# A cached attention layer beside a squared-ReLU layer: two heads a load in 64 KB rows, three places in place of ten

## The chip, the core and the metric

The kernel runs on one of the eight cores of a Trainium2 chip, as one program. The metric is device time in microseconds (us) from launch to end; lower is better. A core has five engines that run side by side, each through its own list of instructions in order: TensorE (PE, matrix products, with its loads of weights as PEld), VectorE (DVE), ScalarE (ACT), GpSimd (POOL) and SyncE (SP, which here only issues transfers). Engines wait for each other by semaphores. Transfers between HBM and the on-chip memory SBUF run on 16 DMA engines. SBUF has 128 partitions; a tile is an array of 128 rows, one in each. Matrix products end up in PSUM.

## The reference

Two tokens (B = 2, one position each) of D = 448 pass through two branches that a gate mixes. Branch A is attention of 16 heads with 256 elements over a cache of 4096 keys and values; branch B is a dense layer with a squared ReLU, 448 to 1792 to 448. All is float32.

```python
g = sigmoid((x * gate_w).sum(-1, keepdims=True))
q = (x @ wq).reshape(B, Sq, H, Dh).transpose(0, 2, 1, 3)
scores = einsum("bhqd,bhkd->bhqk", q, k_cache) * (Dh ** -0.5)
p = softmax(scores, axis=-1)
a = einsum("bhqk,bhkd->bhqd", p, v_cache).transpose(...).reshape(B, Sq, H * Dh) @ wo
h = einsum("bsd,df->bsf", x, w1) + b1
r = where(h > 0, h, 0)
b = einsum("bsf,fd->bsd", r * r, w2) + b2
out = g * a + (1 - g) * b
```

The caches are the bulk of the data: 2 x 16 x 4096 x 256 numbers of 4 bytes, twice, are 268.4 MB. wq and wo are 7.34 MB each, w1 and w2 3.21 MB each.

## The kernel before

**Places.** One pool named `ring` has 10 places of 16 KB a partition (`RING = 10`, `slot`, L54 and L67). Every large load goes to the next place in turn, so it waits until the tile that stood there ten loads earlier has been used up. Almost all loads are 2 MB: 128 rows of 16 KB.

**Order of the loads.** SP issues all large loads, in the order of the program: wq in four pieces (L73), then, pair by pair, keys and values. A pair is one token and one head; there are 32 of them, the two tokens of a head behind each other (`pairs`, L133). The keys of a pair are two loads, its values two more (`load_kv`, L121). In a round i the kernel loads the keys of pair i + 1, then the values of pair i. The weights are strewn in between: w1 at i = 2, half of w2 at i = 4, a quarter of wo at every fourth head, the rest of w2 at the very end. SP also waits at each load for the load eight before it.

**Scores** run on DVE: `times_q` (L268) multiplies 16 keys a partition with the query in place, `row_sums` (L275) sums each key's 256 products. The query lies in all partitions: `make_q` (L218) spreads a row with a matrix product and ACT copies it.

**Softmax** of a pair: DVE takes the maximum m of each partition (L283), PE spreads the 128 maxima to all partitions (mt, L285), DVE takes the maximum of those (nb, L291), ACT computes the exponentials with their sums (L294). While PE makes mt, DVE already multiplies the first four keys of the next pair (`LEAD = 4`). After the second token of a head, PE adds the sums over the partitions and DVE turns them into factors rl (`norm`, L302).

**Values**: `values` (L311) is 16 matrix products of 4 x 512 for a pair, in four column groups of PE, that add up in `po_buf`. [...] `turn` (L320) brings the result of a head into columns, `project` (L333) multiplies it with wo into `acc`.

**Second branch**: `ffn_hidden` (PE and ACT) runs in round 3 behind the values, `ffn_square` (DVE) in round 3 behind the scores of the next pair; the first half of w2 is added to `acc` in round 5, the second half at the end of the program. The end (L406 to L416) adds, behind the last head, five pieces of w2 and the last two blocks of wo to `fin` with narrow products (`late`, L338), copies and writes.

Of the kernel before, what the change touches and what calls it, by code (L numbers as in the profile page):

```python
# [13 lines left out]


@with_exitstack
def kernel(
    ctx: ExitStack,
    tc: tile.TileContext,
    x: bass.AP,  # L20
    k_cache: bass.AP,
    v_cache: bass.AP,
    wq: bass.AP,
    wo: bass.AP,
    w1: bass.AP,
    b1: bass.AP,
    w2: bass.AP,
    b2: bass.AP,
    gate_w: bass.AP,
    out: bass.AP,  # L30
):
    nc = tc.nc
    P = 128
    B, H, S, DH = k_cache.shape
    D = x.shape[-1]
    F = w1.shape[1]
    N = H * DH
    CF = D // P
    R0 = CF * P
    RR = D - R0  # L40
    assert 2 * RR == P and B == 2
    NK = S // P
    J = 16
    NCH = NK // J
    HG = 4
    NG = H // HG
    FC = F // P
    FB = F // D
    NJ = DH // P
    QB = 512  # L50
    NQ = N // QB
    QH = QB // DH
    DQ = D // 4
    RING = 10  # L54
    WH = FC // 2
    LEAD = 4
# [3 lines left out]
    ring = ctx.enter_context(tc.tile_pool(name="ring", bufs=RING))  # L60
    work = ctx.enter_context(tc.tile_pool(name="work", bufs=2))
    ps = ctx.enter_context(tc.tile_pool(name="ps", bufs=2, space=PSUM))
# [4 lines left out]
    def slot(name):  # L67
        return ring.tile([P, J * DH], F32, name=name, tag="ring")


    wq_t = []

    def load_wq():  # L73
        for c in range(CF):
            t = slot(f"wq{c}")
            nc.sync.dma_start(t[:, :N], wq[c * P:(c + 1) * P, :])
            wq_t.append(t)
        t = slot("wqr")
        nc.sync.dma_start(t[:, :N // 2], wq[R0:, :].rearrange("r (s n) -> (r s) n", s=2))
        wq_t.append(t)  # L80

    w1_t = []

    def load_w1():
        ta = slot("w1a")
        tav = ta[:, :2 * F].rearrange("p (c n) -> p c n", c=2)
        nc.sync.dma_start(tav, w1[:2 * P, :].rearrange("(c p) n -> p c n", p=P))
        tb_ = slot("w1b")
        nc.sync.dma_start(tb_[:, :F], w1[2 * P:R0, :])
        nc.sync.dma_start(tb_[:, F:F + F // 2], w1[R0:, :].rearrange("r (s n) -> (r s) n", s=2))  # L90
        w1_t.extend([tav[:, 0, :], tav[:, 1, :], tb_[:, :F], tb_[:, F:F + F // 2]])

    w2_v = w2.rearrange("(p c) n -> p c n", c=FC)
    w2_sb = {}

    def w2_slot(lo, hi):
        t = slot(f"w2_{lo}")
        tv = t[:, :(hi - lo) * D].rearrange("p (c n) -> p c n", n=D)
        for c in range(lo, hi):
            w2_sb[c] = tv[:, c - lo, :]  # L100
        return tv

    def load_w2_early():
        tv = w2_slot(0, WH)
        nc.sync.dma_start(tv, w2_v[:, :WH, :])

    def load_w2_late():
        tv = w2_slot(WH, FC)
        nc.sync.dma_start(tv[:, :FC - 2 - WH, :], w2_v[:, WH:FC - 2, :])
        nc.sync.dma_start(tv[:, FC - 2 - WH:, :], w2_v[:, FC - 2:, :])  # L110

    wo_v = wo.rearrange("(h p j) n -> p h (j n)", p=P, j=NJ)
    wo_sb = {}

    def load_wo(g):
        t = slot(f"wo{g}")
        tv = t[:, :HG * NJ * D].rearrange("p (h k) -> p h k", h=HG)
        nc.sync.dma_start(tv, wo_v[:, g * HG:(g + 1) * HG, :])
        wo_sb[g] = tv.rearrange("p h (j n) -> p h j n", j=NJ)

    def load_kv(src, i, nm, cuts=()):  # L121
        b, h = pairs[i]
        v = src[b, h].rearrange("(n p j) d -> n p j d", p=P, j=J)
        tiles = []
        for n in range(NCH):
            t = slot(f"{nm}{b}_{h}_{n}").rearrange("p (j d) -> p j d", d=DH)
            at = [0, *(cuts if n == NCH - 1 else ()), J]
            for lo, hi in zip(at, at[1:]):
                nc.sync.dma_start(t[:, lo:hi, :], v[n, :, lo:hi, :])
# [314 lines left out]
```

## Time and profile before

| | |
|---|---|
| time, median of 3 runs | 694.6 us (692.71 to 695.77) |
| profiled execution, span | 695.5 us |
| DVE busy | 586.2 us (84%) |
| PE busy | 324.9 us (47%) |
| ACT busy | 41.3 us (6%) |
| HBM read | 289.56 MB, 416 GB/s over the span |
| mean granted clock of TensorE | 0.668 |

The span runs from the first to the last instruction of the profiled execution. The profile page has the busy time of each engine, the span in 40 slices, the DMA queues, the chain of work that ended last, and groups of instructions by line. A window gives the same for a stretch: busy time and count for PE, PEld, DVE, ACT and POOL, then the granted clock of PE as a share of full speed, the busy share of the 16 DMA engines and GB/s. In the timeline each row has a start, a duration and an instruction, and in brackets how long the engine was idle before it and what ended that. A share of busy time is an average over the span; what a stage is worth is read from the wait that ends last in it.

### The profile page before, as it was taken

How to read it: one execution, taken by the hardware profiler on the slowest of the kernel's cores; microseconds unless marked ns; L12 is line 12 of the kernel's file. 1: busy time of each engine (PE TensorE's matmuls, PEld its weight loads, DVE VectorE, ACT ScalarE, POOL GpSimd, SP SyncE). 2: the span in 40 equal slices, each digit the busy share in tenths (PEclk: the TensorE clock that was granted, in tenths of full speed). 3: DMA queues.
4: the chain of work that ended last, by engine and by line, in shares of the span. 5: the costliest groups of instructions: out<-in, count | busy, mean ns of one | idle time of the engine just before them, and what ended most of it. 6: DMA issues, size and time to landing. Idle time of an engine off the chain costs nothing.

```text
span 695.5 us, 4013 instructions
## 1 busy us (share of the span) xinstructions
PE 324.9 (47%) x1570; PEld 88.5 (13%) x1570; DVE 586.2 (84%) x293; ACT 41.3 (6%) x123; POOL 0.7 (0%) x6
## 2 busy tenths in 40 slices
PE   5323244738665244434266245534166453332476
PEld 1000100502111011101011011101011010010022
DVE  2599979099999998997978999899688999999481
ACT  0200000100000000000000000000000000000000
POOL 0000000000000000000000000000000000000000
PEclk9855655767697655665576665566586556765576
DMA  8999999999999999999999999999999999999991
GB/s 363 431 427 427 431 423 427 427 428 422 426 430 428 428 426 428 429 430 421 427 432 424 428 429 429 427 429 421 430 429 429 428 427 428 428 428 428 423 422 72
DMA packets 22446, 289.81 MB, mean 417 GB/s; under 512 B 2454, under 2 KB 2460, under 8 KB 5148
## 3 DMA queue, kind: packets, MB, share of 16 engines
q1 hardware_dynamic: 22264, 289.55, 98.2%
q8 instruction: 12, 0.20, 0.1%
q10 hardware_dynamic: 164, 0.02, 0.0%
q14 instruction: 6, 0.05, 0.0%
HBM read 289.56 MB, written 0.00 MB: 416 GB/s over the span
## 4 chain that ended last, share of the span: by engine, by line
DMA 72%; DVE 17%; PE 7%; ACT 1%; issue 1%; SPq 0%; DVEq 0%; ACTq 0%
DMA k<-in_A_k_cache_dram 42%; DMA v<-in_A_v_cache_dram 25%; DVE k L273 9%; DVE s L279 8%; DMA wo<-in_A_wo_dram 6%; PE po_buf L317 3%; PE pt L248 1%; PE ot L329 1%; PE acc L335 1%; PE ph L242 1%; PE pq L223 1%; ACT o L323 0%; ACT h_sb L244 0%; DVE nb L291 0%; PE fin L340 0%
## 5 line engine op out<-in xcount | busy, mean ns | idle before, releaser
L273 DVE TENSOR_TENSOR k<-k,q 128x4096 f32<-128x4096 f32 (+2 forms) x95 | 287.3, 3025 | 43.6 <-DMA k<-in_A_k_cache_dram 39.2
L317 PE MATMUL po_buf<-v,p 128*4 128x512 f32 x1024 | 198.2, 918 | 228.6 <-DMA v<-in_A_v_cache_dram 226.7
L279 DVE TENSOR_REDUCE s<-k 128x16 f32<-128x4096 f32 x64 | 282.8, 4418 | 2.2
L317 PEld LDWEIGHTS po_buf<-v,p 128*4 128x4 f32 x1024 | 25.8, 102 | 364.2 <-issue 185.7
L285 PE MATMUL mt<-ident,m 128*128 128x128 f32 x64 | 20.1, 407 | 83.8 <-DVE m L283 83.8
L335 PE MATMUL acc<-wo,oT 128*2 128x448 f32 x60 | 29.7, 649 | 0.8 <-ACT oT L331 0.8
L291 DVE TENSOR_REDUCE nb<-mt 128x1 f32<-128x128 f32 x32 | 9.1, 286 | 24.6 <-PE mt L285 24.5
L285 PEld LDWEIGHTS mt<-ident,m 128*128 128x128 f32 x64 | 13.0, 252 | 105.6 <-issue 87.0
L329 PE MATMUL ot<-rl,o 128*128 128x2 f32 x128 | 19.3, 272 | 14.7 <-ACT o L323 14.7
L294 ACT ACTIVATE p<-s,nb 128x32 f32<-128x32 f32 x32 | 10.4, 324 | 263.9 <-DVE nb L291 263.9
L225 ACT ACTIVATE q<-pq 128x512 f32<-128x512 f32 x16 | 9.6, 597 | 212.1 <-PE pq L223 212.1
L329 PEld LDWEIGHTS ot<-rl,o 128*128 128x128 f32 x128 | 17.9, 213 | 32.9 <-ACT o L323 32.9
L299 PE MATMUL sum<-rs,ones_pp 128*128 128x2 f32 x32 | 8.6, 337 | 27.3 <-ACT p L294 27.3
L223 PE MATMUL pq<-qs,ident 128*128 128x512 f32 x32 | 19.2, 686 | 0.0
L323 ACT ACTIVATE o<-po_buf 128x512 f32<-128x512 f32 x16 | 9.5, 595 | 121.3 <-PE po_buf L317 121.3
L253 DVE TENSOR_TENSOR hb<-pt,b1T 128x28 f32<-128x28 f32 x1 | 0.2, 188 | 17.3 <-PE pt L248 17.3
L299 PEld LDWEIGHTS sum<-rs,ones_pp 128*128 128x128 f32 x32 | 7.2, 279 | 31.1 <-ACT p L294 31.1
L212 PE MATMUL po_buf<-wq,xT 128*2 128x512 f32 x48 | 7.8, 804 | 1.9 <-DMA wq<-in_A_wq_dram 1.9
L223 PEld LDWEIGHTS pq<-qs,ident 128*128 128x128 f32 x32 | 5.6, 218 | 20.0 <-issue 19.1
L248 PE MATMUL pt<-ident,h_sb 2*128 2x2 f32 x28 | 7.0, 378 | 2.3 <-ACT h_sb L244 2.3
L335 PEld LDWEIGHTS acc<-wo,oT 128*2 128x2 f32 x60 | 5.0, 92 | 20.4 <-issue 19.4
L248 PEld LDWEIGHTS pt<-ident,h_sb 2*128 2x128 f32 x28 | 6.9, 336 | 3.1 <-ACT h_sb L244 3.1
(60 smaller groups left out, 62.1 us busy)
## 6 DMA issues: line engine op xcount, KB each, us to landing
k<-in_A_k_cache_dram SPq DMA_DIRECT2D x64, 2048.0 KB, 38.7
v<-in_A_v_cache_dram SPq DMA_DIRECT2D x63, 2048.0 KB, 37.7
wo<-in_A_wo_dram SPq DMA_DIRECT2D x4, 1792.0 KB, 37.4
wq<-in_A_wq_dram SPq DMA_DIRECT2D x3, 2048.0 KB, 12.3
v<-in_A_v_cache_dram SPq DMA_DIRECT2D x2, 1024.0 KB, 33.3
w1a<-in_B_w_dram SPq DMA_DIRECT2D x1, 1792.0 KB, 38.6
w<-in_B_w_dram SPq DMA_DIRECT2D x1, 1568.0 KB, 28.9
w<-in_B_w_dram SPq DMA_DIRECT2D x1, 1120.0 KB, 29.9
```

The lines of the kernel that those rows point to most:

```text
L223: nc.tensor.matmul(pq, ident[:, r:r + 1].to_broadcast([P, P]), qs[:, a, :], start=True, stop=True)
L225: nc.scalar.activation(t, pq, AF.Copy)
L248: nc.tensor.matmul(pt[:, c, :], hv[:, c, :], ident[:B, :B], start=True, stop=True)
L273: nc.vector.tensor_tensor(kt, kt, q_sb[b, h].unsqueeze(1).to_broadcast([P, e - a, DH]), op=ALU.mult)
L279: nc.vector.tensor_reduce(s_t[i][:, n * J + a:n * J + e], kts[i][n][:, a:e, :], axis=AX.X, op=ALU.add)
L285: nc.tensor.matmul(mt[:, :P], m.to_broadcast([P, P]), ident, start=True, stop=True)
L294: nc.scalar.activation(p4[b][:, :, 2 * b:2 * b + 2], s_t[i].rearrange("p (m s) -> p m s", s=2), AF.Exp, bias=nb, accum_out=rs_t[h][:, b:b ...
L299: nc.tensor.matmul(sm[:, :B], ones_pp, rs_t[h], start=True, stop=True)
L317: nc.tensor.matmul(po[r:r + 4, :], p4[b][:, m, :], vt[j // J][:, j % J:j % J + 2, :].rearrange("p j d -> p (j d)"), start=(b == 0 and m < ...
L323: nc.scalar.activation(o, po, AF.Copy)
L329: nc.tensor.matmul(ptv[:, j, :], ov[:, s, j, :], rl_t[h][:, :, s], start=(s == 0), stop=(s == 1))
L335: nc.tensor.matmul(acc[:, :D], oT[h][:, j, :], wo_sb[h // HG][:, h % HG, j, :], start=False, stop=(h == H - 2 and j == NJ - 1))
```

## The change

The host hands the weights over laid out by partition: `wq` and `wf` (w1 and w2 side by side) as 128 rows, `wo` as 128 rows in an order of its heads that suits the end, x, the gate's weights and b1 together in one small tensor `pack`. The bytes that are loaded stay about the same.

A round is now one token and **two heads**: head 2t in partitions 0 to 63, head 2t + 1 in 64 to 127, 64 keys a partition. Its keys are one load of 8 MB in rows of 64 KB, its values another. The pool has three places of 64 KB. There are 16 rounds. k of round r + 2 is issued in round r, behind v of round r.

```diff
-    ring = ctx.enter_context(tc.tile_pool(name="ring", bufs=RING))
+    ring = ctx.enter_context(tc.tile_pool(name="ring", bufs=3))
...
+    def place(name):
+        return ring.tile([P, PLACE], F32, name=name, tag="ring")
+
+    def load(t, src, lo, hi):
+        nc.sync.dma_start(t[:, lo:hi], src[:, lo:hi])
+
+    def load_kv(cache, r, name, cuts=()):
+        t, b = rounds[r]
+        tl = place(f"{name}{r}")
+        src = cache[b, 2 * t:2 * t + 2].rearrange("h (p j) d -> (h p) (j d)", j=KEYS)
+        at = [0, *cuts, KEYS]
+        for lo, hi in zip(at, at[1:]):
+            load(tl, src, lo * DH, hi * DH)
+        return tl.rearrange("p (j d) -> p j d", d=DH)
...
+    wqt = place("wq")
+    for lo, hi in ((0, 2 * N), (2 * N, 3 * N + N // 2)):
+        load(wqt, wq, lo, hi)
...
+    cut4 = (KEYS // 4, KEYS // 2, 3 * KEYS // 4)
+    kt[0] = load_kv(k_cache, 0, "k", cut4)
+    wft = place("wf")
...
+    load(wft, wf, 0, CF * F + F // 2)
+    load(wft, wf, CF * F + F // 2, CF * F + F // 2 + FC * D)
+    kt[1] = load_kv(k_cache, 1, "k", cut4)
...
+    def add(lt, rhs):
+        n = added[0]
+        g = n % 4
+        nc.tensor.matmul(acc[32 * g:32 * g + B, :D], lt, rhs, start=n < 4, stop=n >= n_acc - 4)
+        added[0] += 1
...
+    def scores(r, cuts=()):
+        s_t[r] = work.tile([P, KEYS], F32, name=f"s{r}", tag="s")
+        at = [0, *cuts, KEYS]
+        for lo, hi in zip(at, at[1:]):
+            k = kt[r][:, lo:hi, :]
+            nc.vector.tensor_tensor(k, k, q_sb[r].unsqueeze(1).to_broadcast([P, hi - lo, DH]), op=ALU.mult)
+            nc.vector.tensor_reduce(s_t[r][:, lo:hi], k, axis=AX.X, op=ALU.add)
...
+    project_q()
+    make_q(0)
+    half15 = (KEYS // 2, 3 * KEYS // 4, 7 * KEYS // 8)
+    blocks = [(t, k) for t in WO_ORDER for k in range(4)]
+    cuts = (0, 16, 24, 28, 31, 32)
+    for r, (t, b) in enumerate(rounds):
+        scores(r, cut4 if r < 2 else ())
+        if r < R - 1:
+            vt[r] = load_kv(v_cache, r, "v")
+            make_q(r + 1)
+        else:
+            wot = place("wo")
+            for lo, hi in zip(cuts, cuts[1:]):
+                load(wot, wo, lo * D, hi * D)
+        if r > 0:
+            values(r - 1)
+            if b == 0:
+                turn(t - 1)
+        if r == 0:
+            softmax(r)
+            ffn()
+        if r + 2 < R:
+            kt[r + 2] = load_kv(k_cache, r + 2, "k")
+        elif r + 2 == R:
+            vt[R - 1] = load_kv(v_cache, R - 1, "v", half15)
+        if r > 0:
+            softmax(r)
+        if b == B - 1:
+            norm(t)
+    values(R - 1)
+    turn(T - 1)
+    for i, (t, k) in enumerate(blocks):
+        rhs = wot[:, i * D:(i + 1) * D]
+        if i < len(blocks) - LATE:
+            add(o_block(t, k), rhs)
+            continue
...
+        late(wide[:, n, :], rhs, stop=n == LATE - 1)
```

The softmax of a round has one mt for both heads, but two maxima nb, two exponentials (one a half of the partitions) and, in `norm`, two products rl. `values` has 32 matrix products of 8 x 512 a round, the same number in all as before. The second branch (`ffn`) runs whole in round 0, behind its softmax. wo is loaded once, last of all, in five pieces, into the place of the last keys, and all of it is multiplied at the end: 28 blocks into the four column groups of `acc`, the last four into `fin`.

**Where the order moves.** On SP, in the middle of the program before, two pairs with their loads (k or v with its head, its half and a buffer number; DMAHW is the landing of the load eight before, DVE and PE release the place):

```order
L129 DMA k_4_0_576<-in_A_k_cache_dram 128x4096 [waits DMAHW3_49,DVE_49]
L129 DMA k_4_1_578<-in_A_k_cache_dram 128x4096 [waits DMAHW4_49,PE_49]
L129 DMA v_3_0_580<-in_A_v_cache_dram 128x4096 [waits DMAHW5_49,DVE_49]
L129 DMA v_3_1_582<-in_A_v_cache_dram 128x4096 [waits DMAHW6_49,PE_49]
L129 DMA k_4_0_635<-in_A_k_cache_dram 128x4096 [waits DMAHW7_49,PE_49]
L129 DMA k_4_1_637<-in_A_k_cache_dram 128x4096 [waits DMAHW0_49,DVE_49]
L129 DMA v_4_0_639<-in_A_v_cache_dram 128x4096 [waits DMAHW1_49,PE_49]
L129 DMA v_4_1_641<-in_A_v_cache_dram 128x4096 [waits DMAHW2_49,DVE_49]
```

Now, from v of round 0 on (v_183), k of round 2 (k_255), v of round 1 and so on:

```order
L66 DMA v_183<-in_v_cache_dram 128x16384 [waits DMAHW7_49,DMAHW6_49,DVE_49]
L66 DMA k_255<-in_k_cache_dram 128x16384 [waits DMAHW0_49,DMAHW1_49,PE_49,Activation_49]
L66 DMA v_266<-in_v_cache_dram 128x16384 [waits DMAHW4_49,DMAHW3_49,DMAHW5_49,DMAHW2_49,DVE_49]
L66 DMA k_305<-in_k_cache_dram 128x16384 [waits DMAHW6_49,PE_49]
L66 DMA v_327<-in_v_cache_dram 128x16384 [waits DMAHW7_49,DVE_49]
L66 DMA k_375<-in_k_cache_dram 128x16384 [waits DMAHW0_49,PE_49]
```

One load now moves as much as four did. Each v waits for DVE (the scores that empty its place), each k for PE (the values two rounds earlier).

On DVE before, from the maximum of one pair to the end of the next pair's scores (m, nb and s are the tiles of the softmax, k the keys):

```order
L283 TENSOR_REDUCE m_536<-s_524 128x1 [waits DVE_49]
L273 TENSOR_TENSOR k_3_0_528<-k_3_0_528,q_1_369 128x1024 [waits DMAHW7_49]
L291 TENSOR_REDUCE nb_541<-mt_538 128x1 [waits PE_49]
L273 TENSOR_TENSOR k_3_0_528<-k_3_0_528,q_1_369 128x3072
L279 TENSOR_REDUCE s_572<-k_3_0_528 128x16 [waits DVE_49,Activation_49]
L273 TENSOR_TENSOR k_3_1_530<-k_3_1_530,q_1_369 128x4096 [waits DMAHW0_49]
L279 TENSOR_REDUCE s_572<-k_3_1_530 128x16 [waits DVE_49]
```

Now, rounds 3 and 4 (k_305 and k_375):

```order
L184 TENSOR_TENSOR k_305<-k_305,q_332 128x16384 [waits DMAHW6_49,DMAHW1_49,Activation_49]
L185 TENSOR_REDUCE s_386<-k_305 128x64 [waits DVE_49]
L190 TENSOR_REDUCE m_430<-s_386 128x1 [waits DVE_49]
L196 TENSOR_REDUCE nb_434<-mt_432 64x1 [waits PE_49]
L196 TENSOR_REDUCE nb_434<-mt_432 64x1
L210 RECIPROCAL rc_441<-sum_439 128x4 [waits PE_49]
L211 TENSOR_TENSOR rc_441<-rc_441,gP 128x4 [waits DVE_49]
L214 TENSOR_TENSOR rl_444<-m_117,rc_441 128x4 [waits DVE_49]
L214 TENSOR_TENSOR rl_444<-m_117,rc_441 128x4
L184 TENSOR_TENSOR k_375<-k_375,q_394 128x16384 [waits DMAHW3_49,DMAHW0_49,Activation_49]
```

The product of the next keys that stood between m and nb is gone; a pass is two long instructions, which wait for the whole load.

On PE, the end of the program before, from the last values on (w is w2, hT the second branch's hidden row):

```order
L317 MATMUL po_buf_97<-v_15_1_1750,p_1_104 4x512 [waits DMAHW0_49]
L317 MATMUL po_buf_97<-v_15_1_1750,p_1_104 4x512 x3
L329 MATMUL ot_1788<-rl_1768,o_1786 128x2 [waits DVE_49,Activation_49]
L329 MATMUL ot_1788<-rl_1768,o_1786 128x2 x3
L340 MATMUL fin<-w_7_1753,hT 2x112 [waits DMAHW1_49]
L340 MATMUL fin<-w_7_1753,hT 2x112 x19
L340 MATMUL fin<-wo_1655,oT_1793 2x112 [waits Activation_49]
L340 MATMUL fin<-wo_1655,oT_1793 2x112 x7
```

Now (oT are the turned results of two heads each; DMAHW are the pieces of wo):

```order
L223 MATMUL po_103<-v_1113,p_1_113 8x512 x3
L234 MATMUL ot_1219<-rl_1182,o_1217 128x4 [waits DVE_49,Activation_49]
L142 MATMUL acc<-wo,oT_373 2x448 [waits DMAHW7_49]
L142 MATMUL acc<-wo,oT_496 2x448 x4
L142 MATMUL acc<-wo,oT_1224 2x448 [waits DMAHW0_49,Activation_49]
L142 MATMUL acc<-wo,oT_865 2x448 x4
L142 MATMUL acc<-wo,oT_988 2x448 [waits DMAHW1_49]
L147 MATMUL fin<-ya,pick 17x112 [waits Activation_49]
L147 MATMUL fin<-wo,wide 17x112 [waits DMAHW2_49,DVE_49]
L147 MATMUL fin<-wo,wide 17x112 [waits DMAHW3_49,DVE_49]
```

All products with wo now stand behind the last values and behind the last load; none with w2 is left there.

More of the change, by code (lines that the diff above doesn't have):

```diff
@@ L112 @@
[L112 to L129, printed above, removed]
-            tiles.append(t)
-        return tiles
@@ new lines @@
+    values(R - 1)
[5 more added lines that the diff above has]
+            continue
+        n = i - (len(blocks) - LATE)
+        if n == 0:
+            for kk in range(LATE):
+                nc.vector.tensor_copy(wide[:, kk, 0:W:16], o_block(t, kk))
+            ya = const.tile([P, D], F32, name="ya")
+            nc.scalar.activation(ya, acc[:, :D], AF.Copy)
+            late(pick, ya, start=True)
+        late(wide[:, n, :], rhs, stop=n == LATE - 1)
```

450 lines of the change are left out of this document (176 added, 274 removed).

## The prediction

> **What bounds the kernel now.** I read the page from the top (busy shares, 40 slices, queues, chain), then windows of single stretches, then the groups by shape, and last the timeline of the first 30 us and of the end.
>
> ```profile
> span 695.5 us, 4013 instructions
> DMA  8999999999999999999999999999999999999991
> GB/s 363 431 427 427 431 423 427 427 428 422 426 430 428 428 426 428 429 430 421 427 432 424 428 429 429 427 429 421 430 429 429 428 427 428 428 428 428 423 422 72
> q1 hardware_dynamic: 22264, 289.55, 98.2%
> DMA 72%; DVE 17%; PE 7%; ACT 1%; issue 1%; SPq 0%; DVEq 0%; ACTq 0%
> ```
>
> The DMA engines are full from the second slice to the last but one, and 72% of the chain is loads. DVE's 84% is an average that the loads set. So the kernel costs its 289.55 MB over the rate, plus a head and a tail in which little moves. Windows (us, five engines' busy time, clock, DMA share, GB/s) give the rate by row size:
>
> ```profile
> 159.00:162.00 3.00, 2.48 (x14) 0.91 (x18) 3.00 (x1) 0.41 (x2) 0.00 (x0) 0.50 1.01 402
> 321.00:324.00 3.00, 1.77 (x12) 0.37 (x16) 2.97 (x2) 0.00 (x0) 0.00 (x0) 0.50 1.01 402
> 500.00:600.00 100.00, 47.97 (x214) 11.77 (x214) 91.68 (x45) 5.29 (x17) 0.00 (x0) 0.67 1.01 428
> 600.00:640.00 40.00, 16.04 (x80) 3.92 (x80) 37.33 (x18) 2.09 (x7) 0.00 (x0) 0.63 1.01 428
> 682.50:683.00 0.50, 0.50 (x8) 0.03 (x4) 0.29 (x2) 0.00 (x0) 0.00 (x0) 0.50 0.27 90
> 684.00:696.00 12.00, 7.41 (x108) 3.25 (x96) 0.00 (x0) 1.03 (x3) 0.00 (x0) 0.78 0.00 0
> ```
>
> Rows 3 and 4 hold only keys and values in 16 KB rows: 428 GB/s with the engines full. Rows 1 and 2 are loads of wo in 3.5 KB rows: 402, as full. The last bytes move near 683.0; 12.5 us of the span follow.
>
> **What a row costs.** At 402 GB/s over 16 engines a packet of 3584 B takes 142.6 ns; at 428, one of 16384 B takes 612.5 ns. The line through both is 11.0 ns a packet plus 36.71 ns a KB (of 1000 B). A 64 KB packet then takes 2417 ns: 434 GB/s, and 19.33 us for a load of 8.39 MB against 19.60 now. No row shows a 64 KB packet. The bounds are 428 (rows cut up again: no gain) and 436 (no cost per packet at all). I take 434. k2 to k15 and v0 to v14 are 29 such loads: **7.8 us less**.
>
> The Trainium skill, in "DMA: Bandwidth & Descriptors", section "Why small descriptors are slow (HBM only)", gives a packet only about 3 beats of overhead and 32 bytes of metadata. By my estimate from that page, 16 KB rows lose 0.8% and 64 KB rows 0.2%, so 3.4 us would be saved instead of 7.8, and the time would be 682.4, inside the forecast's own range. The two rows above (402 and 428) make a packet dearer than that.
>
> **The head.** wq is the same 7.34 MB in both kernels and starts the queue.
>
> ```profile
> 0.74 1.40 SPq L76 DMA_DIRECT2D wq<-in_A_wq_dram  x3
> 2.29 1.41 PE L177 MATMUL pxt<-ident,x 2*128 2x2 f32 x6 [2.29 <-DMA x<-in_A_x_dram]
> 20.87 1.90 PE L212 MATMUL po_buf<-wqr,xT 128*2 128x512 f32 x16 [0.59 <-DMA wqr<-in_A_wq_dram]
> 25.82 4.42 DVE L273 TENSOR_TENSOR k<-k,q 128x4096 f32<-128x4096 f32 x1 [16.64 <-DMA k<-in_A_k_cache_dram]
> ```
>
> It has landed at 20.8, before and after. The other 282.2 MB at 428 GB/s end at 20.8 + 659.4 = 680.2. Before they end near 683.0, as the narrow rows of w1, w2 and wo are slower: **2.8 us** that wide rows of wf and wo get back. The set-up on DVE (memsets, masks, the gate out of pack) is a dozen short instructions under the load of wq; uncovered it would be 2 to 3 us. With the 7.8 us the last row of wo lands at **672.4**, if the queue never runs dry.
>
> **Does it run dry?** Ten places of 16 KB become three of 64 KB; v of round r takes the place of that round's k. Groups by shape (busy us, mean ns | idle before):
>
> ```profile
> L279 DVE TENSOR_REDUCE s<-k 128x16 f32<-128x4096 f32 x64 | 282.8, 4418 | 2.2
> L273 DVE TENSOR_TENSOR k<-k,q 128x4096 f32<-128x4096 f32 x33 | 145.7, 4416 | 16.6 <-DMA k<-in_A_k_cache_dram 16.6
> L273 DVE TENSOR_TENSOR k<-k,q 128x1024 f32<-128x1024 f32 x31 | 37.8, 1221 | 27.0 <-DMA k<-in_A_k_cache_dram 22.5 <-ACT q L225 4.4
> ```
>
> From 1024 to 4096 elements the product grows by 3195 ns, 1.040 ns each; 16384 elements then take 17.2 us, the row sum as long: a pass of **34.4 us** (35.3 in rounds 0 and 1, in quarters). What lies between passes is read from the end of the trace (start us, us):
>
> ```profile
> 679.65 0.19 DVE L283 TENSOR_REDUCE m<-s 128x1 f32<-128x32 f32 x1
> 679.98 0.77 PE L285 MATMUL mt<-ident,m 128*128 128x128 f32 x2 [5.91 <-DVE m L283]
> 680.79 0.29 DVE L291 TENSOR_REDUCE nb<-mt 128x1 f32<-128x128 f32 x1 [0.95 <-PE mt L285]
> 681.17 0.32 ACT L294 ACTIVATE p<-s,nb 128x32 f32<-128x32 f32 x1 [11.06 <-DVE nb L291]
> 681.40 0.19 ACT L294 ACTIVATION_READ_ACCUMULATOR p<-s,nb 128x1 f32 x1
> 682.16 6.31 PE L317 MATMUL po_buf<-v,p 128*4 128x512 f32 x32
> 682.67 0.16 DVE L307 TENSOR_TENSOR rl<-m,rc 128x4 f32<-128x4 f32 x1
> 688.55 0.60 ACT L323 ACTIVATE o<-po_buf 128x512 f32<-128x512 f32 x1 [6.96 <-PE po_buf L317]
> 689.20 1.11 PE L329 MATMUL ot<-rl,o 128*128 128x2 f32 x8 [0.73 <-ACT o L323]
> 690.23 1.14 PE L340 MATMUL fin<-w,hT 128*2 128x112 f32 x40
> 692.21 0.26 ACT L413 ACTIVATE y<-fin 128x112 f32<-128x112 f32 x1 [1.69 <-PE fin L340]
> 692.50 0.66 SPq L415 DMA_DIRECT2D out_dram<-y  x1
> ```
>
> From m to the end of nb are 1.43 us, plus 0.2 for a second nb: 1.6. The product of the next head that filled this wait is gone, so DVE now stands. Where b is 1, norm follows, and DVE waits for it: 1.75 us from nb to rl, plus 0.5 for the second exp and 0.2 for the second rl: 4.1 in all. So DVE needs 34.4 + 2.85 = **37.3 us a round on average, the queue 38.7**: 1.4 us are left.
>
> The loop over a place: k lands, 34.4 us of pass, v is issued. Issue to landing without the bytes is 1.55 us by the head (0.74 to 2.29) and 3.0 by the end (692.50 to 695.5), the largest price. That is 36 to 37.4 us in a period of 38.7: v is queued 1.3 to 2.7 us before the queue needs it. If the loop is longer, half the excess goes into each round, as v of one round and k of the next but one follow it.
>
> On PE, mt of a round now stands behind the values of the round before. Those are 64 instructions, 12.6 us by the row at 682.16, after a landing 19.3 us past k's, and then 1.9 us of turn: 33.8, just under the pass. An excess falls where b is 0 and DVE has 3 us to spare. SP is in order, so k of round r + 2 also waits behind v of round r; its own release, the values, comes earlier.
>
> **The first rounds.** The second branch now lies in DVE's way, before the scores of round 1.
>
> ```profile
> 124.49 3.17 PE L242 MATMUL ph<-w1a,xT 128*2 128x448 f32 x16
> 127.43 1.89 PE L242 MATMUL ph<-w1b,xT 128*2 128x448 f32 x16
> 129.40 2.18 ACT L244 ACTIVATE h_sb<-ph 2x448 f32<-2x448 f32 x4 [4.63 <-PE ph L242]
> 131.63 6.97 PE L248 MATMUL pt<-ident,h_sb 2*128 2x2 f32 x28 [2.31 <-ACT h_sb L244]
> 138.63 0.19 DVE L253 TENSOR_TENSOR hb<-pt,b1T 128x28 f32<-128x28 f32 x1 [17.30 <-PE pt L248]
> 139.29 0.19 DVE L256 TENSOR_TENSOR hT<-hT,gP 128x28 f32<-128x28 f32 x1
> ```
>
> From ph to hT are 15.0 us; the transposes may now follow the first of four copies, so 13.3. Scores 0 start near 26.3 (25.82 now, for k; q comes up to 1.9 us later, as 32 instead of 16 instructions wait for the last piece of wq) and end at 61.6; mt ends at 62.8, hT at 76.1, scores 1 at 111.4. In the queue k0 (19.6), wf (6.42 MB, 15.0), k1 (19.6), v0 and k2 (19.3 each) land at 40.4, 55.4, 75.0, 94.3 and 113.6, and v1 may be issued at 111.4. The 30 instructions that add the second branch to acc follow hT on PE: 0.197 us each by the row at 682.16 (6.31 for 32), 6 us, so wf's place is free at 82, and k2 needs it at 94: hidden, with 12 us to spare. The place of k1 is free about 1 us before the queue needs it; every us that the branch takes longer is 1 us of idle queue, once. I cost it at nothing, with 0 to 5 us as bounds.
>
> **The tail.** With wo last (17.1 us) behind v15 (19.6) and v14 (19.3), k15 lands 56.0 before the end T = 672.4. Its pass ends at T - 21.6, so the place for wo is free 4 us early; nb, two exps and the sum end at T - 18.3. Values 15 take 12.6 us at half clock, 7.6 at full clock (1.90 us for 16 in the row at 20.87): 10, T - 8.3. Turn: T - 6.4. 56 instructions of 448 columns on wo: 9.7 or 5.8 us, T - 0.6 at best. The last four blocks wait for T anyway; ya (0.5), 40 narrow matmuls (1.1), the copy (0.3) and the write (3.0) follow: T + 4.3 at best, T + 11 at half clock throughout. I take T + 5.6 = **678.0**. Of the tail of 12.5 us, 6.9 go.
>
> Sum against the span of 695.5: 7.8 + 2.8 + 6.9 = 17.5 less. The median of 694.6 lies 0.9 under that span, inside the spread of the three runs (692.71 to 695.77), so 678.0 stands for both.
>
> **Rivals.**
> - *The rows don't stay whole* (the queue cuts them, or the cost a packet hides): 428 GB/s throughout, 680.2 + 5.6 = 685.8, at most 691.5 with the slow tail. For it: no row shows a longer packet. Against: the cost shows between 3.5 and 16 KB. 0.17.
> - *The queue runs dry in the first rounds*, through the second branch or a late v1: up to 10 us once, 683 to 690. The margin is 1 us, and the clock in the branch may be lower. 0.10.
> - *Three places are too few, and DVE becomes the bound*; this one ends slower. The place is every round: each us over 38.7 in pass and gaps costs 15 us. Slower by over 0.5% than 694.6 means 698.1, 20 us more than I forecast, 1.35 a round: it decides from a DVE round of 40.1 on, a pass of 37.2 instead of 34.4. With a pass of 38, 2.2 x 15 = 33 us: 711. For it: DVE has 84%, and its wait for nb is bare. Against: a slope read from 64 rows that agree. 0.07.
> - *Sixteen engines on rows of 64 KB read more slowly.* 29 loads at 402 GB/s (the slowest full row) take 20.87 us each: 45 us more, 723; it decides from 418 GB/s on. Against: 16 KB rows already run at multiples of a power of two, at 428. 0.06.
>
> The Trainium skill, same page, section "Latency and other measured facts", tells of row pitches at large powers of two that slow copies: 512 KiB gave 207 GB/s, 4 MiB half of that, padded rows 214. By its ratio of 207 to 214 my estimate from that page is 415 GB/s and 704 us, which is the last rival. Its pitches are far above 64 KB, and no run here shows the effect.
>
> **How the numbers follow.** The forecast has 0.60, with 673 to 684 of its own: 673.1 is no packet cost at all (20.8 + 282.2/0.4358 + 4.8), 684 the slow tail. The range of 673 to 691 takes in the first two rivals and leaves the last two out. An interval of 0.5% (691.1 to 698.1) is about what a measurement of this kernel can tell from no change. Faster: 0.60 + 0.16 + 0.08 = 0.84; same: 0.01 + 0.02 + 0.02 + 0.01 = 0.06; slower: 0.10.
>
> **What would show it.** Right: full DMA slices at 432 to 434 from 50 us to the end, some 3,600 large packets, DVE products near 17.2 us with waits of 1 to 2 us for k, under 6 us from the last wo row to the end. Wrong: 428 (packets), gaps in the DMA share after 110 us (places), DVE without waits for loads (DVE bound), or PE at half clock behind the last row (tail).

## The result, and the profile after

The changed kernel takes **685.43 us** (median of 4 runs, 685.27 to 686.75), the kernel before on the same chip 694.44 us (median of 4, 692.71 to 695.77): a ratio of 0.988, 95% interval 0.9862 to 0.9899. It is faster, as forecast, and inside the range, but 7.4 us above the forecast of 678.0. In the profiled execution the span is 683.5 us against 695.5, 12.0 less instead of 17.5.

The page of the changed kernel, from the top: span, busy shares, slices, queue, chain, and the two groups of the scores.

```profile
span 683.5 us, 3411 instructions
PE 216.6 (32%) x1452; PEld 62.5 (9%) x1452; DVE 572.1 (84%) x148; ACT 33.2 (5%) x107; POOL 0.7 (0%) x6
DMA  9999999999999999999999999999999999999996
GB/s 383 420 435 423 434 433 454 445 437 426 427 403 433 433 434 430 430 431 433 433 426 434 433 433 433 437 427 418 434 414 433 395 433 434 422 430 419 419 425 278
q1 hardware_dynamic: 7212, 289.54, 98.9%
DMA 50%; DVE 46%; PE 2%; issue 1%; ACT 0%; SPq 0%; DVEq 0%; ACTq 0%
...
L184 DVE TENSOR_TENSOR k<-k,q 128x16384 f32<-128x16384 f32 (+1 forms) x22 | 276.5, 12568 | 41.8 <-DMA k<-in_k_cache_dram 31.4
L185 DVE TENSOR_REDUCE s<-k 128x64 f32<-128x16384 f32 (+1 forms) x22 | 276.4, 12566 | 0.8
```

The queue has 7212 packets instead of 22264 for the same bytes, and the DMA row is full up to the last slice, where it was nearly empty before. But look along the GB/s row: 433 and 434 stand beside 403, 418, 414 and 395. Slices with full engines that move less hold packets that take longer than they should. And the chain has changed its nature: 50% DMA and 46% DVE, a pass and a load taking turns, where 72% was loads alone. That is what a chain looks like when the load waits for the pass. The waits of SP's queue (us in total, times, longest) and a window over the middle 520 us (bounds, length, five engines' busy time, PE's clock, DMA share, GB/s) say it plainly:

```profile
SPq L66 <- DVE m L190: 538.3, 16, 34.8
SPq L66 <- DMA k<-in_k_cache_dram: 67.3, 17, 9.5
115.00:635.00 520.00, 152.77 (x974) 43.67 (x974) 471.64 (x90) 21.37 (x78) 0.00 (x0) 0.61 1.00 428
```

SP stands 16 times at a v until the pass ends, and the rate over the middle is 428 GB/s, what the 16 KB rows gave before. Of the 12 us that were gained, 8.8 come from the tail behind the last landing; the landing itself is only 3.2 us earlier. The head and the tail (timeline; start us, us):

```profile
20.32 3.62 PE L160 MATMUL po<-wq,pk 128*2 128x512 f32 x32 [1.29 <-DMA wq<-in_wq_dram]
25.27 4.43 DVE L184 TENSOR_TENSOR k<-k,q 128x4096 f32<-128x4096 f32 x1 [10.70 <-DMA k<-in_k_cache_dram]
66.88 3.28 PE L263 MATMUL pt<-ident,wf 2*128 2x2 f32 x28 [0.66 <-ACT wf L259]
106.23 0.33 SPq L66 DMA_DIRECT2D v<-in_v_cache_dram  x1
114.60 17.23 DVE L184 TENSOR_TENSOR k<-k,q 128x16384 f32<-128x16384 f32 x1 [5.22 <-DMA k<-in_k_cache_dram]
...
671.62 3.19 PE L142 MATMUL acc<-wo,oT 128*2 128x448 f32 x32
678.64 0.54 ACT L314 ACTIVATE ya<-acc 128x448 f32<-128x448 f32 x1 [6.73 <-PE acc L142]
679.44 0.95 PE L147 MATMUL fin<-wo,wide 128*17 128x112 f32 x32
680.45 0.26 ACT L318 ACTIVATE y<-fin 128x112 f32<-128x112 f32 x1 [1.27 <-PE fin L147]
680.74 0.70 SPq L319 DMA_DIRECT2D out_dram<-y  x1
```

The last piece of wo lands at 679.80, and 3.7 us later all is over; before it was 12.5.

**What the packets show.** The trace has every packet with its start, its time and its bytes. A whole 64 KB row takes 2418 ns (median of 3712; forecast 2417). But 153 packets take more than 0.1 us longer, up to 4.2 us in all, and these are not spread evenly: most are among the first packets of the values, in bursts at 189.8, 345.6, 423.5, 463, 502, 541.5, 581 and 620 us. No burst stands where a k follows a v. Each of those v is issued 1.0 to 2.3 us before its first packet starts; each k some 20 us ahead. In round 3, for example, v is issued when the pass ends, and the next pass starts when the next keys have landed:

```profile
187.79 0.33 SPq L66 DMA_DIRECT2D v<-in_v_cache_dram  x1
192.21 17.22 DVE L184 TENSOR_TENSOR k<-k,q 128x16384 f32<-128x16384 f32 x1 [0.70 <-DMA k<-in_k_cache_dram]
```

These keys land at 192.08 on the last engine, and 2.0 us earlier on the first, which takes its first packet of v at 189.75. So the lead is 1.96 us here. That the engines aren't level is no mark of a late v, though: the landings of one load lie 0.5 us apart at the start, 1.8 at 100 us, at most 3.65 (at 506 us) and 2.1 at the end, and the kernel before ends with 3.7.

So the theory: **v is queued too late**. Not so late that the queue is empty for long (from 115 to 635 us the packets add up to 519.6 us an engine, in the mean), but late enough that its first packets come slow. The rival: slow packets are the price of 64 KB rows or of few places as such, and the lead has nothing to do with it.

### The profile page after: what moved, and what is told of

Read it like the earlier page. It is cut to its first block, busy times and chain, and to the rows that moved or that the text cites. A ratio compares the mean times of both kernels' runs of the same rounds, so it can differ in the third digit from the quotient of the medians.

```text
span 683.5 us, 3411 instructions
## 1 busy us (share of the span) xinstructions
PE 216.6 (32%) x1452; PEld 62.5 (9%) x1452; DVE 572.1 (84%) x148; ACT 33.2 (5%) x107; POOL 0.7 (0%) x6
## 3 DMA queue, kind: packets, MB, share of 16 engines
q1 hardware_dynamic: 7212, 289.54, 98.9%
## 4 chain that ended last, share of the span: by engine, by line
DMA 50%; DVE 46%; PE 2%; issue 1%; ACT 0%; SPq 0%; DVEq 0%; ACTq 0%
DMA k<-in_k_cache_dram 47%; DVE s L185 23%; DVE k L184 23%; DMA wo<-in_wo_dram 3%; PE acc L142 1%; PE ph L254 1%; PE pt L263 0%; DVE m L190 0%; SPq L66 0%; PE mt L192 0%; PE fin L147 0%; ACT p L200 0%; ACT ya L314 0%; ACT wf L259 0%; DVEq L184 0%
## 5 line engine op out<-in xcount | busy, mean ns | idle before, releaser
L184 DVE TENSOR_TENSOR k<-k,q 128x16384 f32<-128x16384 f32 (+1 forms) x22 | 276.5, 12568 | 41.8 <-DMA k<-in_k_cache_dram 31.4
L185 DVE TENSOR_REDUCE s<-k 128x64 f32<-128x16384 f32 (+1 forms) x22 | 276.4, 12566 | 0.8
L223 PE MATMUL po<-v,p 128*8 128x512 f32 x1024 | 147.2, 740 | 318.8 <-DMA v<-in_v_cache_dram 318.8
L223 PEld LDWEIGHTS po<-v,p 128*8 128x8 f32 x1024 | 29.4, 104 | 433.1 <-issue 262.7
L200 ACT ACTIVATE p<-s,nb 64x64 f32<-64x64 f32 x32 | 11.2, 350 | 368.1 <-DVE nb L196 367.7
L172 PE MATMUL pq<-qs,ident 128*64 128x256 f32 x64 | 16.0, 600 | 0.0
L234 PE MATMUL ot<-rl,o 128*128 128x4 f32 x64 | 8.4, 255 | 6.2 <-ACT o L228 6.2
L234 PEld LDWEIGHTS ot<-rl,o 128*128 128x128 f32 x64 | 7.7, 191 | 13.7 <-ACT o L228 13.7
L160 PE MATMUL po<-wq,pk 128*2 128x512 f32 x64 | 8.6, 683 | 1.3 <-DMA wq<-in_wq_dram 1.3
L142 PE MATMUL acc<-wo,oT 128*2 128x448 f32 x56 | 5.8, 538 | 1.1 <-DMA wo<-in_wo_dram 1.1
## 6 DMA issues: line engine op xcount, KB each, us to landing
k<-in_k_cache_dram SPq DMA_DIRECT2D x8, 2048.0 KB, 35.7
```

What stands on the lines that cost most here:

```text
L142: nc.tensor.matmul(acc[32 * g:32 * g + B, :D], lt, rhs, start=n < 4, stop=n >= n_acc - 4)
L160: nc.tensor.matmul(po_bufs[a][32 * gq:32 * gq + B, :], lt, wqt[:, at:at + QB], start=(c == 0), stop=(c == CF))
L172: nc.tensor.matmul(pq[64 * hh:64 * hh + 64, :DH], ident[:, row:row + 1].to_broadcast([P, 64]), qs[:, a, hh * DH:(hh + 1) * DH], start=True ...
L184: nc.vector.tensor_tensor(k, k, q_sb[r].unsqueeze(1).to_broadcast([P, hi - lo, DH]), op=ALU.mult)
L185: nc.vector.tensor_reduce(s_t[r][:, lo:hi], k, axis=AX.X, op=ALU.add)
L200: nc.scalar.activation(p8[b][z, :, c:c + 3:2], s_t[r][z].rearrange("p (m s) -> p m s", s=2), AF.Exp, bias=nb[z], accum_out=rsm[t % 2][z, h ...
```

## The experiments

The kernel before, timed beside each group of experiments, had medians of 694.0 to 694.8 us, so their times can be set side by side. Times are medians; where only one is given, it is of one run.

### The first four: smaller places, a shorter pass, shorter rows, another end

**Half places.** Six places of 32 KB, so that v's first half may go when the first half of the keys is used up:

```diff
-    PLACE = KEYS * DH
+    HALF = KEYS // 2
+    PLACE = HALF * DH
-    ring = ctx.enter_context(tc.tile_pool(name="ring", bufs=3))
+    ring = ctx.enter_context(tc.tile_pool(name="ring", bufs=6))
```

> Six places of 32 KB in place of three of 64 KB; every 8 MB of keys or values is two loads in 32 KB rows, and a pass runs in two halves, so the first half of v can be issued some 17 us before the pass ends. Theory (v is issued only 1 to 2 us before the queue needs it, its first packets come slow, and the engines that fall behind hold up the next k): no slow packets at the turn from k to v, keys land every 38.8 us (4 x 9.71), the last row of wo lands near 675.7 instead of 679.8, time about 681. Rival (the slow packets belong to any turn of the queue, or to the moment of the softmax, whenever v was issued): the same stretches stay slow, keys land every 39.2 us as now, time 685 to 687.

Measured: 684.1 us (683.63 to 684.65, 5 runs; ratio 0.9849, 0.9829 to 0.9869). Slow packets are gone: 13 behind 110 us, where the changed kernel has some 150. But rows are now 32 KB, and the middle runs at 431 GB/s. The mechanism is as the theory has it, the gain (1.3 us) is between the two forecasts; it can't decide alone.

**A shorter pass.** The scores of 8 of the 64 keys a partition are left out from round 2 on; nothing else moves, and v goes 4.3 us earlier.

```diff
-        at = [0, *cuts, KEYS]
+        at = [0, *cuts, KEYS] if cuts else [0, KEYS - 8]
+        if not cuts:
+            nc.vector.memset(s_t[r][:, KEYS - 8:], -1000.0)
```

> From round 2 on the scores of 8 of the 64 keys in a partition are left out (set to -1000), all loads stay as they are: the pass is 4.3 us shorter, v is issued 5 to 6 us before the queue needs it. Theory (late v): the slow packets go, keys land every 38.7 us, the last row of wo near 674, time about 679.5. Rival (slow packets at any turn, or rows of 64 KB by themselves): time stays at 685. If it is DVE that bounds the rounds, time falls too, but then the wait of DVE for k stays near zero; by the theory it grows to 5 us a round.

Measured in one run: 681.85 us. 11 slow packets instead of 153, loads that land 19.36 us apart from 76 to 560 us. DVE's wait for keys doubles (68.7 us after 31.4), so the time saved on DVE itself bought nothing: it is v's start that paid.

**Rows of 16 KB.** Keys and values in four loads each, in the three places:

```diff
-            vt[r] = load_kv(v_cache, r, "v")
+            vt[r] = load_kv(v_cache, r, "v", cut4)
-            kt[r + 2] = load_kv(k_cache, r + 2, "k")
+            kt[r + 2] = load_kv(k_cache, r + 2, "k", cut4)
```

> Same three places and the same order, but every load of keys and values is cut into four of 16 KB rows. Theory of the packet (11 ns each): a clean 8 MB take 19.6 us instead of 19.36, 7 us more over 29 loads; a part of that (up to 3 us) comes back, as v is then issued earlier against the queue: 689 to 692. Rival (the cost of a packet hides, rows of 64 KB bring nothing): 685.

Measured in one run: 688.7 us; a packet of 16 KB takes 614 ns, a load 19.62 us. Waits of SP and the window over the middle:

```profile
SPq L66 <- DMA v<-in_v_cache_dram: 280.3, 16, 20.5
SPq L66 <- DVE m L190: 177.1, 15, 25.6
SPq L66 <- PE po L223: 38.2, 14, 3.6
115.00:635.00 520.00, 190.36 (x990) 44.84 (x990) 468.37 (x90) 21.38 (x78) 0.00 (x0) 0.62 1.01 427
```

More had changed than the rows: SP now waits 14 times for PE, which the changed kernel never does in the middle. The pool had handed out its places otherwise: v goes where the values of the round before stood, and k where the keys had been. So v is issued well ahead here (at 137.3, with the keys before it landing at 154), and there are no bursts of slow packets. This is the price of 16 KB rows alone, with nothing late.

**The end as it was: wo ahead of the last values.**

```diff
         elif r + 2 == R:
-            vt[R - 1] = load_kv(v_cache, R - 1, "v", half15)
+            wot = place("wo")
+            for lo, hi in zip(cuts, cuts[1:]):
+                load(wot, wo, lo * D, hi * D)
...
+            values(R - 1)
+            turn(T - 1)
```

> wo is loaded ahead of v15, and its blocks of heads 0 to 13 are added ahead of the last values; behind the last load stand a quarter of the last values, turn and the last four blocks. Theory (wo last leaves the shortest chain behind the last byte): 3.7 us from the last landing to the end become 7 to 8, time 688 to 690. Rival (the write of the output and its latency make the tail, whatever stands there): 685 to 686.

Measured in one run: 693.0 us, above both. Two things are mixed in it: a longer tail (last landing 683.56, end 691.2, so 7.6 us), and last values that can be issued only when the last pass ends, at 659.31, so that the last landing is 3.8 us later too. It was made again below, without the second.

### A place for v alone

Two places for keys, one for values, and v's load written behind the matmuls that free it:

```diff
+    def home(name):
...
+        kind, r = name[0], int(name[1:])
+        if kind == "k":
+            return (1, 0)[r] if r < 2 else 2 - r % 2
+        if r == R - 1:
+            return 2
+        return 1 if r == 0 else 0
...
-        return ring.tile([P, PLACE], F32, name=name, tag="ring")
+        return ring.tile([P, PLACE], F32, name=name, tag=f"ring{home(name)}")
...
         if r > 0:
             values(r - 1)
             if b == 0:
                 turn(t - 1)
+        if 2 <= r < R - 1:
+            vt[r] = load_kv(v_cache, r, "v")
```

> 64 KB rows and three places as after the change, but from round 2 on the values have a place of their own (values of round r go where those of round r-1 were, keys of round r+2 where the keys of round r were), so that v is issued behind the matmuls of the values before it, some 15 us ahead of the queue's need, and no longer at the end of a pass. Nothing else in the loads' order or sizes changes. Theory (v issued 1 to 2.3 us before the queues run out makes the first packets slow and the engines drift apart): slow 64 KB packets go (excess under 1.5 us an engine where the changed kernel has 5.3), every load lands 19.36 us behind the one before but for single late engines, last wo piece at about 675, time 681.5 us (679.5 to 683). Rival (the drift is the price of 64 KB rows as such, or of sharing places at all): 685 to 686, with slow packets as in the changed kernel.

Measured: **681.26 us** (681.09 to 681.37, 5 runs; ratio 0.9795, 0.9771 to 0.9819). The bytes, rows and order are those of the changed kernel. Slow packets: 11. The page's slices, SP's waits, the middle, the end:

```profile
GB/s 382 420 432 425 449 432 429 432 432 433 437 432 432 432 432 433 433 433 432 436 432 437 436 440 436 440 429 432 429 432 432 432 432 429 432 436 429 415 427 253
```

```profile
SPq L78 <- DMA v<-in_v_cache_dram: 325.3, 14, 24.8
SPq L78 <- DVE m L202: 128.6, 15, 29.6
SPq L78 <- PE po L235: 126.9, 14, 9.7
```

```profile
115.00:635.00 520.00, 149.49 (x974) 43.24 (x974) 475.38 (x90) 21.38 (x78) 0.00 (x0) 0.61 1.00 432
```

```profile
675.37 0.95 PE L159 MATMUL fin<-wo,wide 128*17 128x112 f32 x32
676.67 0.70 SPq L334 DMA_DIRECT2D out_dram<-y  x1
```

The dips in the GB/s row are gone. v is now held by PE and goes 7 to 8 us ahead. That is less than the 15 us of the expectation, since the matmuls that free its place (32 products, 64 instructions in the trace) take 9.15 us from the landing of the values before (134.03 to 143.18, the first 4.4 us of it at half clock). From 115 to 635 us the packets, which overlap a little, add up to 520.8 us an engine, 1.2 more than in the changed kernel: there some engines had stood empty at the turns as well. The softmax still falls on the first packets of v here (the maximum at 149.27, the first packet at 150.94), so it isn't what slows them. The last piece of wo lands at 675.77 instead of 679.80. This version beats both kernels; it is the changed kernel's own idea with one load issued earlier. The half places fit as well: two packets of 32 KB (1216 ns each) take 11 ns more than one of 64 KB (2421 here), 2.6 us over the 29 loads, and 681.3 + 2.6 = 683.9 is what they took (684.1).

### The lead, up and down

A second sum of 4 keys makes each pass 1.22 us longer. It was put on the changed kernel and on the one above.

```diff
+        if r > 1:
+            nc.vector.tensor_reduce(s_t[r][:, :4], kt[r][:, :4, :], axis=AX.X, op=ALU.add)
```

> The changed kernel with a second sum of 4 of the 64 keys behind each pass from round 2 on (same values written again): the pass is some 1.08 us longer, 35.5 instead of 34.5 us, and v is issued that much later. DVE has the time by itself: 35.5 + 1.65 or + 4.2 us between passes is 38.45 us in the mean, under the 38.72 us of two loads. Theory (the lead of v decides): lead falls from 1.0-2.3 to about 0-1.2 us, more and slower first packets at each of 13 turns, about 0.5 us a turn more: 691 us (688 to 697). Rival (lead does not matter, the pass is hidden): 685 to 686.5.

> The same second sum of 4 keys added to the kernel with a place of its own for the values. Theory: k is issued some 20 us ahead and v does not hang on the pass, so the longer pass is hidden: within 1 us of that kernel (681.5 to 682.5). Rival (the second sum costs by itself, through DVE or the SBUF that DMA and DVE share): as much slower than that kernel as the long pass makes the changed kernel.

Measured: with the place of its own 681.57 us (681.08 to 681.97, 4 runs), hidden, as expected. On the changed kernel **681.29 us** (681.17 to 681.57, 4 runs): more work made it *faster*, against theory and rival. The waits of SP in that kernel give the reason:

```profile
SPq L66 <- DMA v<-in_v_cache_dram: 308.0, 14, 26.9
SPq L66 <- DVE m L192: 144.8, 15, 29.9
SPq L66 <- PE po L225: 129.6, 14, 10.0
```

The pool had changed the places again, as with the 16 KB rows: v waits for PE and goes early. So this run says nothing of a longer pass with a late v; it is a second version with early values. The test was made again with the places held: three names in turn, which is where the pool put them in the changed kernel, as a control; then the second sum on that; then the control with the scores of 2 of the 64 keys left out.

```diff
-        return ring.tile([P, PLACE], F32, name=name, tag="ring")
+        n = turns[0] % 3
+        turns[0] += 1
+        return ring.tile([P, PLACE], F32, name=name, tag=f"ring{n}")
```

> Control: the changed kernel with its three places given in turn by hand (wq, k0, wf, k1, v0, k2, v1, ...), which is where the pool put them by itself, so every load is issued as in the changed kernel (v at the end of a pass). Both theories: 685.4 us (684.5 to 686.8), slow packets as before, excess about 5 us an engine.

> The control with a second sum of 4 of the 64 keys behind each pass (1.22 us in the run before). There the pool had changed the places when the sum was added, and v came early; here the places are held, so v is issued 1.22 us later than in the control. DVE's own time (pass 35.7 and a mean gap of 2.9 us between passes) stays under two loads of 19.36. Theory (the lead of v decides): lead from 1.0-2.3 down to about 0-1.1 us, slow packets in every one of 13 turns, 0.5 us a turn more than the control: 691 us (688 to 697). Rival (the lead does not matter, it was the place of v that mattered in some other way): within 1 us of the control.

> The control with the scores of 2 of the 64 keys a partition left out from round 2 on (set to -1000): the pass is 1.08 us shorter and v is issued that much earlier, 2.1 to 3.4 us ahead, which is about the length of one 64 KB packet (2.42 us). Theory: slow packets mostly gone, excess 1 to 2.5 us an engine, 682.5 us (681.3 to 684). Rival (lead does not matter): 685.

Measured: control 685.78 us (684.45 to 687.37, 4 runs); longer pass 693.63 (692.38 to 695.14, 10 runs; ratio to before 0.9984, 0.997 to 0.9998); shorter pass 681.23 (681.06 to 681.26, 4 runs). The windows over the middle, in the order control, longer, shorter:

```profile
115.00:635.00 520.00, 153.06 (x974) 43.64 (x974) 471.04 (x90) 21.37 (x78) 0.00 (x0) 0.61 1.00 428
```

```profile
115.00:635.00 520.00, 152.59 (x974) 43.66 (x974) 479.35 (x103) 21.38 (x78) 0.00 (x0) 0.61 0.99 422
```

```profile
115.00:635.00 520.00, 152.69 (x974) 43.68 (x974) 461.81 (x103) 21.40 (x78) 0.00 (x0) 0.61 1.00 432
```

With the 64 KB packets of the profiled execution (lead: from the issue of a v, v2 to v14, to the start of its earliest packet; packets over 0.1 us longer than the median; what all packets took above the median, as a mean per engine). The time is the median of all runs; the profiled ones of the first three rows took 695.14, 685.27 and 687.07 us:

| kernel | lead, us | slow packets | excess, us | time, us |
|---|---|---|---|---|
| places held, pass 1.22 us longer | 0.96 to 1.9 | 210 | 8.3 | 693.63 |
| changed kernel | 0.97 to 2.3 | 153 | 5.3 | 685.43 |
| places held (control) | 0.96 to 2.6 | 156 | 5.5 | 685.78 |
| places held, pass 1.08 us shorter | 1.8 to 2.8 | 32 | 1.3 | 681.23 |
| pass 4.3 us shorter (one run) | 4.5 to 6.1 | 11 | 0.8 | 681.85 |
| v in a place of its own | 7.1 to 8.3 | 11 | 0.8 | 681.26 |

1.08 us of lead are worth 4.6 us, and a further 5 us nothing. In the other direction 1.22 us cost 7.9 us, 0.6 for each of the 13 turns. In six of these turns the lead is 0.96 to 0.99 us, the least that is seen: there the fastest engines had run dry. So the 7.9 us are not slow packets alone: from 115 to 635 us the packets add up to 514.7 us an engine, 4.9 less than in the control, and three passes start 0.24 to 0.80 us after their keys have landed, as DVE is still at the norm before (1.8 us in all). The kernel with a place of its own bears the same second sum at 0.3 us. The theory holds, with empty engines beside the slow packets; the rival falls.

The last run asked whether the lead counts in us or in packets: the control, with the last 8 keys of each k as a load of its own in 8 KB rows, so that several short packets stand ahead of v.

```diff
-            kt[r + 2] = load_kv(k_cache, r + 2, "k")
+            kt[r + 2] = load_kv(k_cache, r + 2, "k", (KEYS - 8,))
```

> The control (places held in turn, v at the end of a pass, 1.0 to 2.6 us before its first packet starts), with the keys of rounds 2 to 15 in two loads: rows of 56 KB, and 8 rows of 8 KB an engine behind them, so that what is still ahead in the queue when v is issued is several short packets instead of one long one. The lead in us stays. The short rows cost 8 x 11 ns a load, 1.2 us in all. If the lead has to be counted in packets (an engine must have its next packet's orders before it begins the last one): slow packets mostly gone, 682.5 us (681.8 to 684). If it counts in us: as the control plus the short rows, 686.5 (685.3 to 688.5).

Measured: 684.89 us (682.59 to 687.52, 4 runs). Of its 1920 packets of 64 KB 112 are slow, at leads of 1.0 to 2.5 us. So short packets ahead don't cure it. But the time lies between the two forecasts, the slow packets are fewer than the control's 156, and the runs lie 5 us apart: a partial help isn't excluded, and the question stays open.

### The end's order, with nothing late

The kernel with v's own place, wo loaded where the keys of round 14 were and the values of round 15 behind it; the program's end as in the run with the values last.

```diff
+            wot = place("wo")
+            for lo, hi in zip(cuts, cuts[1:]):
+                load(wot, wo, lo * D, hi * D)
...
-            wot = place("wo")
-            for lo, hi in zip(cuts, cuts[1:]):
-                load(wot, wo, lo * D, hi * D)
+            vt[R - 1] = load_kv(v_cache, R - 1, "v", half15)
```

> The kernel with a place of its own for the values, with wo loaded ahead of the last values instead of behind them (wo where the keys of round 14 were, the last values where those of round 14 were; sums of heads 0 to 13 before the last values). All loads stay issued over 10 us ahead, so this is the price of the end's order alone, which the kernel with values last and late v could not give. Behind the last landing stand then 8 value matmuls (1.04 us), the copy of o (0.60), the turn (1.05), oT (0.18), four copies (0.38), 32 matmuls of wo (1.16), y (0.26) and the output, 7.6 us from landing to end in that run against 3.6 in the kernel with its own place. Theory: bytes and last landing as there (675.8), end 683.4, time 685.2 us (684.3 to 686.3). Rival (the tail is hidden by late engines): 681.3 to 682.

Measured: 687.28 us (685.7 to 687.39, 4 runs). The last landing is 675.75, as in the kernel it is compared with (675.77); the end comes at 685.6 instead of 679.4. Its timeline from there:

```profile
675.79 1.90 PE L233 MATMUL po<-v,p 128*8 128x512 f32 x8 [1.44 <-DMA v<-in_v_cache_dram]
677.82 0.60 ACT L238 ACTIVATE o<-po 128x512 f32<-128x512 f32 x1 [12.24 <-PE po L233]
678.47 1.87 PE L244 MATMUL ot<-rl,o 128*128 128x4 f32 x8 [0.78 <-ACT o L238]
680.81 1.70 PE L157 MATMUL fin<-wo,wide 128*17 128x112 f32 x32 [0.47 <-DVE wide L328]
682.57 0.26 ACT L331 ACTIVATE y<-fin 128x112 f32<-128x112 f32 x1 [2.02 <-PE fin L157]
```

The four steps that stand behind a value's landing but not behind a row of wo (the last matmuls, the copy of o, the turn, the copies of oT) cost 6.2 us of span, two more than expected: PE's clock is 0.50 over this stretch, where it was 0.76 in the earlier run, and its work takes 5.5 us instead of 3.3 (1.90 us for the 8 matmuls that took 1.04).

## Why the prediction was right, and where its size was off

In the terms of the profiled execution the forecast was a last landing at 672.4 and an end at 678.0; measured were 679.80 and 683.5. The direction was right. But 685.43 lies above the 673 to 684 that the prediction gave to its own mechanism; it is in the range of 673 to 691 because that left room for two rivals, and neither of them happened. To that extent it was luck that the range held.

- **The price of a packet: right.** 2418 to 2421 ns against 2417. With v early, loads land 19.36 us apart (forecast 19.33). Rows of 16 KB against 64 KB, both with early values, are 688.7 against 681.26, so 7.4 us; the forecast had 7.8. By the estimate from the Trainium skill ("DMA: Bandwidth & Descriptors", section "Why small descriptors are slow (HBM only)") it would have been 3.4: the runs bear out the price that the two rows of before gave. The rival of rows that don't stay whole fell with the 3712 packets of 64 KB. Its sign, 428 GB/s, came up all the same, for another reason. The rival of slow 64 KB rows fell with the 434 GB/s of single slices; the rule of the Trainium skill on pitches (same page, "Latency and other measured facts") has no effect to be seen at 64 KB.
- **Three places: the step that failed.** "v is queued 1.3 to 2.7 us before the queue needs it" was counted up to the landing of the keys ahead: 38.7 - 34.4 = 4.3 us from issue to that landing, less 1.55 to 3.0. The 4.3 came out (187.79 to 192.08 in round 3). But the first engine is done with those keys, and wants v, 2.3 us before they have landed on the last. So from issue to first packet there are only 0.97 to 2.3 us, and 0.96 is what it takes where engines have run dry: 0 to 1.3 us of room are left. That so little room costs nothing was wrong as well: with a lead of 1.0 to 2.3 us the first packets come slow and some engines stand empty, the next keys land later, and with them the next pass and the next v. From the first 64 KB packet to the end of the last are 569.1 us; with v in its own place 564.6. That is **4.5 us**, and it took most of what the long rows gave in the middle: 428 GB/s over it, as before the change.
- **The other 3.4 us of the landing** stand in the kernel with its own place too (675.77). There the keys of round 1 land 0.5 later than forecast (75.54), the 29 loads take 2.4 longer (v14 lands at 638.54; the 2421 ns of a packet make 1.0 of it), v15 and wo 0.4. A single engine is late there, for which see the last section: of the 16 landings the last comes 1.0 us behind the fifteenth, at 75.54 as at 638.54. No run tried its part alone.
- **The first rounds: right, with more room than thought.** Scores 0 start at 25.27 (26.3), v1 is issued at 106.23 (111.4). The 28 transposes take 3.28 us, not 6.97. No queue ran dry there; that rival fell.
- **The pass: right.** 17.23 + 17.22 us, forecast 34.4. DVE waits 31.4 us for keys, so it isn't the bound; but DVE's end of pass sets v, so the pass sits in the chain all the same. The rival in which three places make the kernel slower had the right place and set the limit too late: by its sum a pass of 35.7 us still costs nothing (35.7 + 2.85 = 38.55 a round, under 38.7), but 1.22 us more of pass bring the time back to 693.63, though DVE still waits 26.0 us for keys there.
- **The tail: right, and mis-sized in the kernel's favour.** 3.7 us instead of 5.6. That the order of the last loads is what pays was tested: 6.2 us of span when it is turned round.
- **Span and time.** The sum let 678.0 stand for both. The profiled executions here have a time of 1.8 us over their span (685.27 and 683.5, 681.21 and 679.4). Put together: 678.0 + 3.4 + 4.0 (the later landing, 679.80 against 675.77) - 1.9 (tail) = 683.5, and 1.8 more is the 685.3 of that execution.

## What to carry to other kernels

A queue whose engines look full in every slice can still be fed too late. The engines are not level, so the first one wants the next load before the last has landed the one ahead. For each load, look how long before its first packet it is issued (1.8 to 2.8 us were enough here, 1.0 to 2.3 were not). If its place is released by the slowest engine's last instruction, give it a place that something earlier frees. That cost nothing here and was worth 4 us. And where a pool hands out places by itself, read the waits of the issuing queue before the time of an experiment, since an edit elsewhere can turn the places over.

## What the runs showed of the hardware that was not expected

- A load that is issued 1 to 2.3 us before its first packet starts has some first packets of 2.5 to 4.2 us where 2.42 is the rule, in bursts over several engines; at 4.5 us or more none. Why they are slow is open. Short packets ahead (684.89 us, 112 slow ones) did not cure it.
- Each run fetches instructions in packets of 16 KB on a queue of its own (q8: 11 packets, 0.18 MB in the changed kernel). The kernel with v's own place has just 11 slow 64 KB packets, scattered one by one, each some 0.4 to 0.7 us longer. In its trace each of them starts as such a packet ends: eight behind a fetch of q8 (102.98 + 1.10 us, and the slow packet at 104.06), three behind an 8 KB packet of q14, the second queue of that kind (158.50 + 0.33, and 158.82). So a fetch costs its engine its own 1.0 to 1.1 us and half a us more, and that engine then stays behind: the 16 landings of a load are 2.0 us apart at 150 us, 3.15 behind the fetch at 563.96, and 3.5 at the end. The kernel before has them too. No run left the fetches out.
- The second branch's transposes take 3.28 us for 28 instructions where they took 6.97. The columns that PE loads lie side by side now, not 14 apart. PE's clock isn't the reason: it was full for the first 3 us of the 6.97, and one transpose followed the other after 244 ns there as later at half clock, against 111 ns now. No run changed the columns alone.
